# Key features of two batches in one block, joined GpSimd sums, and a factor moved to PSUM, in an attention and ELU kernel on one Trainium2 core

## The chip, the cores and the metric

The kernel runs on one core of a Trainium2 chip. The metric is the device time of one execution in microseconds. Before the change it is 264.04 us, the median of three runs (263.98 to 265.52).

## The reference

Two stages, all in float32 in effect (inputs that arrive in a wider type are rounded on the chip):

```python
def phi(x):                                    # r = 8
    a = einsum('rd,bhsd->bhsr', S1, x)
    b = einsum('rd,bhsd->bhsr', S2, x)
    return einsum('bhsi,bhsj->bhsij', a, b).reshape(..., 64)
q_p, k_p = phi(q), phi(k)                      # q, k, v: 4 batches, 4 heads, 1088 rows, 32 wide
kv = einsum('bhsf,bhsd->bhfd', k_p, v)
z  = sum(k_p, axis=2)
x  = einsum('bhsf,bhfd->bhsd', q_p, kv) / (einsum('bhsf,bhf->bhs', q_p, z) + 1e-6)
x  = x.transpose(0, 2, 1, 3).reshape(4352, 128)
h  = x @ w_in                                  # 128 -> 2048
g  = where(h > 0, h, exp(min(h, 0)) - 1)
out = g @ w_out                                # 2048 -> 128
```

## The kernel before, in words

The 4352 rows are cut into nine groups: groups 0 to 7 have 512 rows each (two to a batch), group 8 has the 256 left over. The 2048 hidden columns are cut into eight pairs `cp` of 128-column chunks. A step of the main loop (L1047) is one pair (group, cp), numbered n. Steps 2 to 15 take groups 0 and 1 alternately, steps 16 to 23 group 2, 24 to 31 group 3, 32 to 39 group 4, and so on to step 63; group 8 has a loop of its own at the end (L1090).

The schedule is written out by hand: each engine runs its instructions in the order in which the program issues them. A step n issues, in this order:

1. `mm1` (L787), TensorE: both halves c0 and c1 of h, 512 columns each, into two of the four banks of the PSUM tag `h`. So step n uses the banks of step n-2.
2. what was filed for the step with `at(n, ...)`.
3. `elu` of half 0: two ScalarE activations make e from h (L808, L810), one VectorE instruction makes gg from e and h (L816).
4. what was filed with `mid(n, ...)`.
5. `elu` of half 1.
6. what was filed with `late(n, ...)`.
7. the second matmul of step n-2, from its gg.

From step 14 on the second matmul is `mm2_seven` (L717), a scheme with seven products of half-size blocks in place of eight. Three of its operands are plain quarters of gg and the other four are sums of quarters, `tt` (t0 to t3), which GpSimd makes in `sums7` (L690): t0 after half 0, then t2, t1 (from t2) and t3 (from t1) after half 1. The products are issued as p1, p2, p3, p5 (t0), p7 (t2), p6 (t1), p4 (t3); in the first and last step of a group p6 and p3 come third and fourth.

The attention stage is spread over the same steps. For batches 1 to 3 the key side is: `transp` (L279) transposes the loaded keys on VectorE; `KF_late` (L353) computes the key features on TensorE, as eight matmuls on array tiles of 64 by 32, into two banks of the PSUM tag `aux` (two banks in all); `KF_late_out` (L365) empties them with two VectorE transposes into `abk`; `KO_a` and `KO_b` form the outer products (L378, L386); `KA` (L422) sums keys times values; `turn` and `turned` finish z. The loop at L993 files these under the steps in its table: `n_t` for the transpose, `n_f` for the key features.

The query side: `queries(g5, g1, n)` (L655) is a TensorE block in step n-1 that computes the numerators of group g5 (L642) and the query features of group g1 (L536), into the two h banks of step n and two `aux` banks (`qps`). In step 22 it does the numerators of group 3 and the features of groups 4 and 5. Before that, for group 3, `q2_den` (L555) makes the denominators on VectorE (pw, den, an), `q2_half` (L620) the outer product qp from an and abw (L625), and `q4` (L628) transposes qp. For groups 4 to 7 `q2_a` (L614) first copies an into an `aux` bank with ScalarE (tile `qa`), and `q2_half` reads it from there.

The buffers that matter: `kT` and `qT` have two buffers each, shared by batches 0 and 2 and by 1 and 3; `abk` has two; `gg` three; `tt` shares a tag of five.

Of the kernel before, what the change touches and what calls it, by code (L numbers as in the profile page):

```python
# [12 lines left out]
F32 = mybir.dt.float32  # L13
ALU = mybir.AluOpType
U32 = mybir.dt.uint32
MUL, ADD, SUB, MAX = ALU.mult, ALU.add, ALU.subtract, ALU.max
# [6 lines left out]
def _ap(ap: bass.AP, free):  # L23
    return dataclasses.replace(ap, ap=[list(ap.ap[0])] + [list(x) for x in free])
# [3 lines left out]
def kernel(  # L28
# [21 lines left out]
    nc = tc.nc  # L50
    B, H, S, D = q.shape
    R = S1.shape[0]
    P = 128
# [4 lines left out]
    NT = S // 64  # L58
# [7 lines left out]
    psum = ctx.enter_context(tc.tile_pool(name="psum", bufs=2, space=bass.MemoryType.PSUM))  # L66
# [5 lines left out]
    kT = [const.tile([FD, 2 * KT, 64], F32, name=f"kT{b}") for b in range(2)] * 2  # L72
    qT = [const.tile([FD, NT, 64], F32, name=f"qT{b}") for b in range(2)] * 2
# [276 lines left out]

    def KF_late(b):  # L353
        ps = [psum.tile([P, 512], F32, name="kfps", tag="aux") for _ in range(2)]
        for c in range(4):
            u, w = divmod(c, 2)
            for g2 in range(2):
                r = slice(64 * g2, 64 * g2 + 64)
                nc.tensor.matmul(ps[g2][32 * c:32 * c + 32, :32 * KT],  # L359
                                 Sxp[r].rearrange("p x c r -> p (x c r)"),  # L360
                                 kT[b][r, u * KT:u * KT + KT, 32 * w:32 * w + 32],
                                 skip_group_check=True, tile_position=(64 * g2, 32 * c))
        feats[b] = ps
# [303 lines left out]
    hs, es, gs, ops = {}, {}, {}, {}  # L667
# [19 lines left out]
    def quarter(g, cp, c, y):  # L687
        return gs[g, cp][:, c].rearrange("p (u x s) -> p u x s", u=2, x=2)[:, :, y, :]

    def sums7(g, cp, c):  # L690
        if c == 0:
            ts[g, cp] = work.tile([P, 4, 2, P], F32, name="tt", tag="raw", bufs=5)
        t = ts[g, cp]
        b11, b12 = (quarter(g, cp, 0, y) for y in range(2))
        if c == 0:
            nc.gpsimd.tensor_tensor(t[:, 0], b12, b11, op=SUB)  # L696
            return
        b21, b22 = (quarter(g, cp, 1, y) for y in range(2))
        nc.gpsimd.tensor_tensor(t[:, 2], b22, b12, op=SUB)  # L699
        nc.gpsimd.tensor_tensor(t[:, 1], t[:, 2], b11, op=ADD)  # L700
        nc.gpsimd.tensor_tensor(t[:, 3], b21, t[:, 1], op=SUB)  # L701

# [248 lines left out]
    steps = [(0, 0), (0, 1), (1, 0), (1, 1)] + [(g, cp) for cp in range(2, NP - 2) for g in range(2)]  # L951
# [6 lines left out]
    def at(n, f, *a):  # L958
        extra.setdefault(n, []).append((f, *a))

    def mid(n, f, *a):
        extra.setdefault((n, 0), []).append((f, *a))

    def late(n, f, *a):
        extra.setdefault((n, 1), []).append((f, *a))
# [25 lines left out]


    for b, (n_t, n_f, n_o, n_a, n_z) in enumerate(  # L993
            ((4, 6, (7, 9), 11, 12), (15, 16, (17, 18), 19, 20), (19, 21, (23, 24), 27, 28)), 1):
        at(n_t, transp, kT, "k", b, 0, NT)
        at(n_f, KF_late, b)
        late(n_f, KF_late_out, b)
        for half in range(2):
            if b == 1:
                at(n_o[half], KO, b, half, nc.gpsimd)  # L1000
            else:
                late(n_o[half] - 1, KO_a, b, half)
                at(n_o[half], KO_b, b, half)
        at(n_a, KA, b)
        late(n_a, sums_out, b)
        at(n_z, turn, b)
        at(n_z, turned, b)
    late(10, transp, qT, "q", 1, 0, NT)
    at(21, transp, qT, "q", 2, 0, NT)
    late(24, transp, qT, "q", 3, 0, NT)  # L1010

    for n, g, nx in ((13, None, 2), (15, 2, 3), (22, 3, 4), (30, 4, 6), (46, 6, 8), (62, 8, None)):
# [8 lines left out]
    late(13, q2_half, 2, 0)  # L1021
    mid(14, q4, 2)
    late(19, q2_den, 3)
    late(19, q2_half, 3, 0)
    late(20, q4, 3)
    late(22, q2_den, 4)
# [20 lines left out]
    for n in range(2, N):  # L1047
        g, cp = steps[n]
# [6 lines left out]
        if seven(g, cp):  # L1055
            sums7(g, cp, 0)
# [15 lines left out]
        if seven(g, cp):  # L1072
            sums7(g, cp, 1)
# [4 lines left out]
        g, cp = before  # L1078
# [10 lines left out]
    g = NQ - 2  # L1089
# [53 lines left out]
```

## Time and profile before

| | us |
|---|---|
| median of three runs | 264.04 |
| profiled execution, its own time | 264.85 |
| span of the profiled execution, first to last instruction | 262.9 |
| mean of one gg instruction (L816), 128 of them | 0.682 |
| mean of one GpSimd sum (L696, L699, L700, L701), 50 of each | 0.735, 0.737, 0.731, 0.760 |
| mean of one stored-key transpose of 1088 columns (L280) | 1.311 |

The profile is of one execution. Busy times of the engines overlap, and a share of the span is an average over stages. The engines are PE (TensorE; PEld is its weight loading, which overlaps), DVE (VectorE), ACT (ScalarE), POOL (GpSimd) and SP, which issues transfers. PE can count as busy while a matmul waits for its bank, so a wait of PE is looked for in the start times and in the weight loads, too. The granted TensorE clock has a mean of 0.998 of full speed.

### The profile page before, as it was taken

The numbers are of one execution on the slowest core, as the hardware profiler recorded it, in microseconds if no ns is written. First come the engines' busy times: TensorE is split into PE (matmuls) and PEld (weight loads), VectorE is DVE, ScalarE is ACT, GpSimd is POOL, SyncE is SP. The second block draws the span as 40 slices with busy tenths as digits, with TensorE's granted clock in tenths as the row PEclk, the third lists the DMA queues.
The fourth block names the chain that finished last, engine by engine and source line by source line (L and its number), as shares of the span: only waits on it lengthen the run. The fifth ranks groups of instructions, "written<-read, shape, count | busy, mean of one in ns | idle before, by whom it ended". The sixth has DMA issues, their size and how long they took to land.

```text
span 262.9 us, 9941 instructions
## 1 busy us (share of the span) xinstructions
PE 257.1 (98%) x4219; PEld 159.2 (61%) x4219; DVE 188.2 (72%) x355; ACT 182.9 (70%) x356; POOL 169.2 (64%) x253
## 2 busy tenths in 40 slices
PE   8899999999999999999999999999999999999994
PEld 6652333354346746667666666665666666667994
DVE  5899999997969997996477676644456445673651
ACT  2469878677567655784687777776777777777793
POOL 4420008205387996798868799898689888997300
PEclk9999999999999999999999999999999999999999
DMA  5998079012011210001100200011001100110021
GB/s 171 326 353 220 7 235 268 7 36 78 12 24 26 33 38 3 5 15 26 35 0 4 30 13 2 0 29 15 5 0 17 27 4 0 24 21 2 0 32 33
DMA packets 28507, 14.30 MB, mean 54 GB/s; under 512 B 21392, under 2 KB 26640, under 8 KB 28464
## 3 DMA queue, kind: packets, MB, share of 16 engines
q1 hardware_dynamic: 28032, 13.32, 20.6%
q8 instruction: 33, 0.54, 0.9%
q10 hardware_dynamic: 368, 0.30, 0.3%
q14 instruction: 10, 0.08, 0.1%
q0 software_dynamic: 64, 0.07, 0.1%
HBM read 11.31 MB, written 2.36 MB: 52 GB/s over the span
## 4 chain that ended last, share of the span: by engine, by line
PE 94%; DMA 2%; DVE 1%; ACT 0%; issue 0%; ACTq 0%; DVEq 0%
PE h L256 45%; PE pb L737 17%; PE pa L737 13%; PE o L256 5%; PE pb L713 4%; PE ol L256 3%; DMA hd_k<-in_k_dram 2%; PE h L642 1%; PE kv L427 1%; PE qps L642 1%; PE kfps L359 1%; PE h L536 1%; PE qtp L595 1%; DVE qp L583 0%; PE xps L602 0%; PE abp L340 0%
## 5 line engine op out<-in xcount | busy, mean ns | idle before, releaser
L256 PE MATMUL h<-xg,W 128*32 128x512 f32 (+3 forms) x904 | 130.9, 540 | 0.4 <-ACT xg L608 0.4
L816 DVE SCALAR_TENSOR_TENSOR gg<-e,h 128x512 f32<-128x512 f32 x128 | 85.5, 682 | 52.6 <-ACT e L810 51.3
L808 ACT ACTIVATE e<-h 128x512 f32<-128x512 f32 x128 | 75.5, 590 | 47.0 <-PE h L256 46.0
L810 ACT ACTIVATE e<-e 128x512 f32<-128x512 f32 x128 | 80.9, 632 | 3.8
L256 PEld LDWEIGHTS h<-xg,W 128*32 128x32 f32 (+1 forms) x904 | 43.1, 122 | 43.2 <-issue 34.0
L699 POOL TENSOR_TENSOR tt<-gg 128x256 f32<-128x256 f32 x50 | 36.8, 737 | 16.3 <-DVE gg L816 16.1
L696 POOL TENSOR_TENSOR tt<-gg 128x256 f32<-128x256 f32 x50 | 36.7, 735 | 6.5 <-DVE gg L816 6.2
L701 POOL TENSOR_TENSOR tt<-gg,tt 128x256 f32<-128x256 f32 x50 | 38.0, 760 | 3.9
L700 POOL TENSOR_TENSOR tt<-tt,gg 128x256 f32<-128x256 f32 x50 | 36.6, 731 | 3.9
L737 PEld LDWEIGHTS pa<-gg,W 128*64 128x64 f32 (+1 forms) x496 | 23.9, 126 | 23.7 <-issue 23.0
L737 PE MATMUL pa<-gg,W 128*64 128x128 f32 (+1 forms) x496 | 30.7, 274 | 0.0
L737 PE MATMUL pb<-tt,SS 128*64 128x128 f32 (+1 forms) x480 | 29.6, 273 | 0.0
L737 PEld LDWEIGHTS pb<-tt,SS 128*64 128x64 f32 (+1 forms) x480 | 22.8, 126 | 0.0
L737 PE MATMUL pa<-tt,SS 128*32 128x128 f32 (+1 forms) x288 | 21.2, 273 | 0.0
L737 PE MATMUL pb<-tt,W 128*64 128x128 f32 (+1 forms) x256 | 20.2, 273 | 0.2 <-issue 0.2
L737 PE MATMUL pb<-gg,SS 128*64 128x128 f32 (+1 forms) x256 | 19.9, 273 | 0.0
L134 POOL TENSOR_TENSOR raw<-raw,tiny 128x512 f32<-128x512 f32 x1 | 1.0, 1042 | 24.7 <-DVE raw L129 24.7
L256 PE MATMUL o<-gg,W 128*32 128x512 f32 x128 | 15.3, 595 | 0.0
L737 PEld LDWEIGHTS pa<-tt,SS 128*32 128x32 f32 (+1 forms) x288 | 13.7, 124 | 0.0
L737 PEld LDWEIGHTS pb<-tt,W 128*64 128x64 f32 (+1 forms) x256 | 12.8, 125 | 0.5 <-issue 0.5
L737 PEld LDWEIGHTS pb<-gg,SS 128*64 128x64 f32 (+1 forms) x256 | 12.8, 125 | 0.0
L713 PE MATMUL pb<-gg,W 128*32 128x256 f32 x192 | 11.6, 380 | 0.0
(154 smaller groups left out, 285.2 us busy)
## 6 DMA issues: line engine op xcount, KB each, us to landing
raw<-in_moe_w_in_dram SPq DMA_DIRECT2D x8, 256.0 KB, 6.3
raw<-in_moe_w_out_dram SPq DMA_DIRECT2D x8, 256.0 KB, 6.6
out_dram<-ob SPq DMA_DIRECT2D x112, 16.0 KB, 1.5
hd_k<-in_k_dram SPq DMA_DIRECT2D x3, 544.0 KB, 6.8
hd_q<-in_q_dram SPq DMA_DIRECT2D x3, 544.0 KB, 8.2
v<-in_v_dram SPq DMA_DIRECT2D x4, 288.0 KB, 7.0
v<-in_v_dram SPq DMA_DIRECT2D x4, 256.0 KB, 8.6
kvs<-kvd SPq DMA_DIRECT2D x13, 32.0 KB, 1.9
```

Source lines behind the costliest of these rows:

```text
L256: nc.tensor.matmul(dst[c:c + tile], lhs[:, c:c + tile], rhs, skip_group_check=True, tile_position=(0, c), **kw)
L359: nc.tensor.matmul(ps[g2][32 * c:32 * c + 32, :32 * KT], Sxp[r].rearrange("p x c r -> p (x c r)"), kT[b][r, u * KT:u * KT + KT, 32 * w:32 ...
L642: nc.tensor.matmul(ps[w][32 * r:32 * r + 32, :64 * n], kvs[b][rows, r, f, :], qpT[g, i][rows, o:o + 2 * n, f, :], start=(f == 0), stop=(f ...
L696: nc.gpsimd.tensor_tensor(t[:, 0], b12, b11, op=SUB)
L699: nc.gpsimd.tensor_tensor(t[:, 2], b22, b12, op=SUB)
L700: nc.gpsimd.tensor_tensor(t[:, 1], t[:, 2], b11, op=ADD)
L701: nc.gpsimd.tensor_tensor(t[:, 3], b21, t[:, 1], op=SUB)
L713: nc.tensor.matmul(acc[1][0][r:r + width[0], 256 * hi:256 * hi + 256], lhs[:, w:w + width[0]], gg[:, c, 256 * u:256 * u + 256], start=(cp ...
L737: nc.tensor.matmul(bank[r:r + width[0], P * col:P * col + P], lhs[:, w:w + width[0]], rhs[:, u], start=(first and i in ((0,) if g == 1 els ...
L808: nc.scalar.activation(e, hs[g, cp][c][:, :n], RELU, scale=-1.0)
L810: nc.scalar.activation(e, e, EXP, scale=-1.0)
L816: nc.vector.scalar_tensor_tensor(gs[g, cp][:, c, :n], es[g, cp][:, c, :n], -1.0, hs[g, cp][c][:, :n], op0=ADD, op1=MAX)
```

## The change

Four edits. The key features of batch 3 move from step 21 to step 16, right behind those of batch 2; they go into the two h banks of step 17 instead of `aux` banks, and are emptied between the two halves of step 16. The transposes of loads move with them: batch 2's keys from step 15 to the end of step 12, batch 3's keys from step 19 to step 15, batch 2's queries from step 21 to step 19. GpSimd's t0 and t2 become one instruction after half 1, so that each step has three GpSimd sums in place of four. And group 3's factor an is copied into an `aux` bank by ScalarE, as that of the later groups is.

```diff
-    def KF_late(b):
-        ps = [psum.tile([P, 512], F32, name="kfps", tag="aux") for _ in range(2)]
+    def KF_late(b, n=None):
+        if n is None:
+            ps = [psum.tile([P, 512], F32, name="kfps", tag="aux") for _ in range(2)]
+        else:
+            ps = hs[steps[n]] = [psum.tile([P, 512], F32, name="h", tag="h", bufs=4) for c in range(2)]
...
-        b11, b12 = (quarter(g, cp, 0, y) for y in range(2))
         if c == 0:
-            nc.gpsimd.tensor_tensor(t[:, 0], b12, b11, op=SUB)
             return
-        b21, b22 = (quarter(g, cp, 1, y) for y in range(2))
-        nc.gpsimd.tensor_tensor(t[:, 2], b22, b12, op=SUB)
+        b11, b21 = quarter(g, cp, 0, 0), quarter(g, cp, 1, 0)
+        us = [[2 * P, 2], [1, P]]
+        nc.gpsimd.tensor_tensor(_ap(t[:, 0], [[4 * P, 2], [P, 2], [1, P]]), _ap(gs[g, cp][:, 0, P:], [[4 * P, 2]] + us),
+                                _ap(gs[g, cp][:, 0], [[P, 2]] + us), op=SUB)
         nc.gpsimd.tensor_tensor(t[:, 1], t[:, 2], b11, op=ADD)
         nc.gpsimd.tensor_tensor(t[:, 3], b21, t[:, 1], op=SUB)
...
-            ((4, 6, (7, 9), 11, 12), (15, 16, (17, 18), 19, 20), (19, 21, (23, 24), 27, 28)), 1):
-        at(n_t, transp, kT, "k", b, 0, NT)
-        at(n_f, KF_late, b)
-        late(n_f, KF_late_out, b)
+            ((4, 6, (7, 9), 11, 12), (12, 16, (17, 18), 19, 20), (15, 16, (23, 24), 27, 28)), 1):
+        (late if b == 2 else at)(n_t, transp, kT, "k", b, 0, NT)
+        at(n_f, KF_late, b, n_f + 1 if b == 3 else None)
+        (mid if b == 3 else late)(n_f, KF_late_out, b)
...
-    at(21, transp, qT, "q", 2, 0, NT)
+    at(19, transp, qT, "q", 2, 0, NT)
...
     late(19, q2_den, 3)
+    late(19, q2_a, 3, 0)
     late(19, q2_half, 3, 0)
```

## Prediction

> **What bounds the kernel now.** I read the page's busy times first, then the chain of waits, then the four engines' timelines from 60 to 125 us, where everything that the change touches lies. "Step" is the index n of the step loop; c0 and c1 are the two halves of a step.
>
> ```profile
> span 262.9 us, 9941 instructions
> PE 257.1 (98%) x4219; PEld 159.2 (61%) x4219; DVE 188.2 (72%) x355; ACT 182.9 (70%) x356; POOL 169.2 (64%) x253
> ```
>
> PE is busy 98% of the span, and the chain of waits gives it 94%. A plain step is 1.72 us of `mm1` (L256) and 1.52 of seven products (L737): the starts 105.72, 108.97 and 112.21 are 3.24 apart. So only two kinds of edit can move the end: fewer PE instructions or changes of tile shape, and waits that hide inside "busy" PE. Timeline of PE, then its weight loads (start, duration, instruction; the bracket is a wait and what ended it):
>
> ```profile
> 92.45 1.94 PE L256 MATMUL h<-xg,W 128*32 128x512 f32 x16
> 94.32 0.71 PE L359 MATMUL kfps<-kT,Sxp 64*32 64x288 f32 x16
> 94.96 0.64 PE L737 MATMUL pa<-gg,W 128*32 128x128 f32 x16
> ...
> 98.35 0.65 PE L642 MATMUL h<-qpT,kvs 32*32 32x128 f32 x4
> 98.98 0.66 PE L642 MATMUL qps<-qpT,kvs 32*32 32x128 f32 x3
> ...
> 100.93 0.64 PE L737 MATMUL pa<-gg,W 128*32 128x128 f32 x16
> ```
>
> ```profile
> 98.98 0.13 PEld L642 LDWEIGHTS qps<-qpT,kvs 32*32 32x32 f32 x2 [0.26 <-DVE abk L369]
> 99.35 0.10 PEld L642 LDWEIGHTS qps<-qpT,kvs 32*32 32x32 f32 x1 [0.23 <-DVE abk L369]
> ```
>
> This is step 21 and the `queries` block of step 22. That block wants the two `aux` banks that `KF_late(3)` filled in step 21, and VectorE empties them (abk, L369) only at 98.47 to 99.29. It takes 100.93 - 98.35 = 2.58 us. The block of step 15 (three rounds of 128 columns, 71.06 to 72.47) takes 1.41, that of step 30 (three of 256, 128.81 to 130.87) 2.06; this one has two rounds of 128 and one of 256, so 1.41 + 0.65/3 = 1.63. The stall is 2.58 - 1.63 = 0.95 us. Why VectorE is late:
>
> ```profile
> 88.41 1.26 DVE L816 SCALAR_TENSOR_TENSOR gg<-e,h 128x512 f32<-128x512 f32 x2
> 89.58 0.24 DVE L436 STREAM_TRANSPOSE kvt<-kv 128x64 f32<-128x64 f32 x1
> 89.73 0.82 DVE L560 TENSOR_TENSOR pw<-abw 128x128 f32<-128x128 f32 x1
> 90.58 0.30 DVE L567 TENSOR_REDUCE den<-pw 128x16 f32<-128x144 f32 x1
> 90.92 0.25 DVE L568 RECIPROCAL den<-den 128x16 f32<-128x16 f32 x1
> 91.21 0.78 DVE L570 TENSOR_TENSOR an<-abw,den 128x128 f32<-128x128 f32 x1
> 92.02 1.71 DVE L625 TENSOR_TENSOR qp<-an,abw 128x1024 f32<-128x1024 f32 x1
> ...
> 94.94 1.23 DVE L632 STREAM_TRANSPOSE qpT<-qp 128x1024 f32<-128x1024 f32 x1
> 96.11 1.27 DVE L280 STREAM_TRANSPOSE qT<-hd_q 128x1088 f32<-128x1088 f32 x1
> 97.30 1.24 DVE L816 SCALAR_TENSOR_TENSOR gg<-e,h 128x512 f32<-128x512 f32 x2
> 98.47 0.82 DVE L369 STREAM_TRANSPOSE abk<-kfps 128x288 f32<-128x288 f32 x2
> ```
>
> Its timeline marks no idle time from 81.82 to 99.87. Three rows are long: the same pw and an took 0.28 and 0.29 in step 14 (66.17, 67.10), and qp took 1.23 there.
>
> **Part by part.** *Batch 3's key features in step 16.* Step 21 loses its block: `mm1` would end at 92.45 + 1.72 = 94.17, the products start at 94.96 (and run 0.03 longer), so 0.82 us. Of that, 288 columns at `mm1`'s rate (1.72 us for two rounds of 512) are 0.48; the rest is the change of tile shape. In step 16 the second block follows one of the same shape, so it adds 0.48, at most 0.64 (the block's own start to the next start). PE: -0.34. Its banks are step 17's h banks, read last by step 15's gg, which ends near 75.2, before PE gets there at 76.69. Their emptying (0.84) moves between step 16's two gg: PE is done near 77.17, gg c0 near 77.23, the transposes near 78.1; `mm1` of step 17 needs the banks at 78.24 + 0.48 = 78.72. Hidden by 0.6 us; beyond that PE waits one for one. Everything after is 0.48 later with PE.
>
> *The four transposes of loads.* Batch 2's keys (1.3 us) go into VectorE's idle 1.50 before gg at 64.16: free; without that gap gg of step 13 slips a few tenths, and PE wants its banks only at 69.2. Batch 3's keys take the old place of batch 2's, batch 2's queries that of batch 3's keys: equal lengths, nothing. What counts is that the 1.27 at 96.11 is gone. The loads were issued by SP at 33.57 to 36.09 and land a median 6.8 (keys) and 8.2 us (queries) later; no later load waits for the freed buffers, so SP's queue does not move.
>
> *The stall in step 22.* KF's two banks are out of the way, so the block waits only for gg of step 21 (its h banks). Now follow VectorE with the third edit, group 3's factor in PSUM. pw starts at 89.73 + 0.48 = 90.21; with the trace's own excess an ends at 90.21 + 2.26 = 92.47. A new wait follows: the ScalarE copy `qa` stands in ScalarE's queue ahead of step 20's two exponentials and waits for an. The same shape of handover (abk to ka to kp, 79.21 to 79.57) costs 0.36: qp starts at 92.83 and takes 1.18 (the rows that read qa: 1.18 at 115.07, 1.21 at 117.37), end 94.01, against 93.73 + 0.48 = 94.21 before. ScalarE is free at 92.78, so e of step 20 is there at 94.04 and 95.19 (1.26 and 2.41 after the start, as from 90.28); gg 20 ends 95.88 (`mm1` of step 22 needs it near 97.03); qpT to 97.0; e of step 21 at 97.5, gg 21 c1 ends near 98.2. PE reaches the block at 98.35 + 0.48 - 0.82 = 98.01: a stall of 0.2. Bounds: without any excess on pw and an, an ends at 91.43 and there is no stall; with a whole joined GpSimd sum (1.29, below) before each of the two, an ends at 90.21 + 1.22 + 2.58 = 94.0 and the stall is near 1.75. I take 0.2, the row's own excess.
>
> *GpSimd's sums joined.* GpSimd's rows grow evenly: 128x128 0.46, 128x192 0.60, 128x256 0.735, so 128x512 is 0.735 + 256 x 2.15 ns = 1.29; the one two-input 128x512 row (L135) is 1.31. Two sums of 0.735 become one of 1.29: 0.18 us less in each of 50 steps, 9 us off an engine that is not on the chain. But the sum on c0 no longer starts early, and the last result comes 1.29 - 0.735 = 0.55 later after gg c1. Cover, step by step: in a plain step t3 would be ready at 209.66 against a use at 211.99 or later; the tightest are step 23 (t1 ready 110.0, used 111.12) and the last step (t1 244.92, used 246.06), where 1.1 us shrinks to 0.6. Zero on the path; a further 0.6 of delay would make PE wait one for one. In step 19 the joined sum also meets VectorE:
>
> ```profile
> 89.67 0.73 POOL L701 TENSOR_TENSOR tt<-gg,tt 128x256 f32<-128x256 f32 x1
> 90.36 0.79 POOL L696 TENSOR_TENSOR tt<-gg 128x256 f32<-128x256 f32 x1
> 91.11 0.73 POOL L699 TENSOR_TENSOR tt<-gg 128x256 f32<-128x256 f32 x1
> 91.92 0.73 POOL L700 TENSOR_TENSOR tt<-tt,gg 128x256 f32<-128x256 f32 x1
> 92.73 1.60 POOL L701 TENSOR_TENSOR tt<-gg,tt 128x256 f32<-128x256 f32 x1
> ```
>
> pw, an and qp end 0.15, 0.15 and 1.08 us after a GpSimd sum has ended, and the sum at 92.73 lasts as long as qp. The Trainium skill, SBUF — State Buffer, "Who interferes with whom", says that a VectorE instruction with two SBUF inputs and a GpSimd instruction that reads SBUF exclude each other for a whole instruction, whoever starts first. That speaks against joining: by it the longest wait grows from 0.73 to 1.29, and with both waits at the longest the sum would be the upper bound above rather than the 0.2. It speaks for the factor in PSUM.
>
> Sum: -0.82 + 0.48 - 0.95 + 0.2 = -1.09 us. The profiled execution took 264.85 (span 262.9 and 1.95 around it), so it would take 263.76; it lies 0.81 above the median, and the median of 264.04 becomes 262.95, say 263.0.
>
> **Rivals.** *ScalarE's new wait (slower).* If an ends later than 92.47 + 1.09 = 93.56, the e of steps 20 and 21, held behind `qa`, make the block of step 22 wait over 1.3 us, and the kernel is slower than before. At the bound of 94.0: -0.34 - 0.95 + 1.75 = +0.46, 264.5. For it: both waits of VectorE are in the trace already and the sums get longer. Against: it needs two nearly full waits.
>
> *The wait stays in another form.* One full wait gives a stall near 0.95, and only PE's 0.34 is gained: 263.7. For it: gg of step 21 ends at 98.54 already in the trace.
>
> *GpSimd becomes the bound.* A step then costs the joined sum plus 1.62 (the starts 203.51, 204.32, 205.13 and 0.73). Above 1.62 us for the joined sum that exceeds 3.24; at 1.75 some 46 steps lose 0.13 each, 6 us, 270. Against: all widths of the trace lie on one line, and even two old sums end to end are 1.47.
>
> **How the numbers follow.** Forecast (262.7 to 263.4) 0.68, stall kept (263.4 to 263.9) 0.14, ScalarE's wait 0.12, GpSimd 0.04, and 0.02 for a larger gain than PE's idle time shows. Range: from the no-stall end, 264.04 - 1.29 = 262.75, less 0.25 for the scatter of the runs, to 264.2, inside the slower rival. One per cent, 2.6 us, is about what tells a difference from none; only GpSimd's rival reaches it: faster 0.02, same 0.94, slower 0.04.
>
> **What would show it.** Two kfps/h blocks of 0.64 + 0.48 back to back near 76; `mm1` of step 17 without a wait; no block in step 21; the queries block near 1.6 to 1.9 us, its wait now on gg; `qa` right behind an; qp near 1.2; the joined sum near 1.29 and the seven products every 3.24 us. Wrong if the products wait for tt, or if PE waits over 1.3 us in step 22.

## The result and the profile after

| | before | after |
|---|---|---|
| median of eleven runs each, us | 264.07 | 263.41 |
| lowest and highest | 263.75, 265.76 | 263.0, 263.75 |
| profiled execution, its own time | 264.85 | 263.75 |
| its span | 262.9 | 261.9 |

The ratio is 0.9964, with a 95% interval of 0.9947 to 0.9981: between 0.5 and 1.4 us less. The forecast was 263.0, inside a range of 262.5 to 264.2, and "no change beyond 1%" had 0.94. The part of the range that had 0.68 ends at 263.4, so 263.41 lies just above it, in the part of the rival "stall kept"; the timelines below show that the stall was not kept. The two profiled executions differ by 1.10 us against a working of 1.09. That fit is closer than the working deserves, as the ledger below shows.

The head of the page after the change:

```profile
span 261.9 us, 9901 instructions
PE 256.3 (98%) x4219; PEld 160.3 (61%) x4219; DVE 188.5 (72%) x355; ACT 183.1 (70%) x357; POOL 161.3 (62%) x203
...
L701 POOL TENSOR_TENSOR tt<-gg 128x512 f32<-128x512 f32 x50 | 64.3, 1285 | 29.8 <-DVE gg L819 23.5
```

GpSimd is busy 161.3 us instead of 169.2, with 50 instructions fewer; the joined sum takes 1.285 us. PE makes the same 4219 matmuls. The timeline of PE in steps 16, 21 and 22 (start, duration, instruction):

```profile
76.08 0.71 PE L362 MATMUL kfps<-kT,Sxp 64*32 64x288 f32 x16
76.59 0.69 PE L362 MATMUL h<-kT,Sxp 64*32 64x288 f32 x16
77.21 0.42 PE L740 MATMUL pa<-gg,W 128*32 128x128 f32 x8
...
78.77 1.90 PE L256 MATMUL h<-xg,W 128*32 128x512 f32 x16
...
93.28 1.89 PE L256 MATMUL h<-xg,W 128*32 128x512 f32 x14
94.79 0.70 PE L740 MATMUL pa<-gg,W 128*32 128x128 f32 x14
...
96.52 1.89 PE L256 MATMUL h<-xg,W 128*32 128x512 f32 x14
98.34 0.40 PE L645 MATMUL h<-qpT,kvs 32*32 32x128 f32 x2
...
100.05 0.65 PE L740 MATMUL pa<-gg,W 128*32 128x128 f32 x16
```

In step 16 the two blocks of key features follow each other, in step 21 there is none between `mm1` and the products, and the queries block of step 22 takes 100.05 - 98.34 = 1.71 us instead of 2.58. No wait for `abk` is left in it. The timeline of VectorE from step 19's gg to step 21's:

```profile
88.93 1.26 DVE L819 SCALAR_TENSOR_TENSOR gg<-e,h 128x512 f32<-128x512 f32 x2
90.10 0.23 DVE L439 STREAM_TRANSPOSE kvt<-kv 128x64 f32<-128x64 f32 x1
90.25 0.41 DVE L563 TENSOR_TENSOR pw<-abw 128x128 f32<-128x128 f32 x1
...
91.31 1.39 DVE L573 TENSOR_TENSOR an<-abw,den 128x128 f32<-128x128 f32 x1
93.04 1.23 DVE L628 TENSOR_TENSOR qp<-qa,abw 128x1024 f32<-128x1024 f32 x1 [0.34 <-ACT qa L621]
...
95.38 0.69 DVE L819 SCALAR_TENSOR_TENSOR gg<-e,h 128x512 f32<-128x512 f32 x1 [0.39 <-ACT e L813]
95.98 1.24 DVE L635 STREAM_TRANSPOSE qpT<-qp 128x1024 f32<-128x1024 f32 x1
97.14 1.25 DVE L819 SCALAR_TENSOR_TENSOR gg<-e,h 128x512 f32<-128x512 f32 x2
```

And GpSimd's, beside an:

```profile
91.28 1.28 POOL L701 TENSOR_TENSOR tt<-gg 128x512 f32<-128x512 f32 x1
92.63 0.73 POOL L703 TENSOR_TENSOR tt<-tt,gg 128x256 f32<-128x256 f32 x1
```

Where before pw took 0.82, an 0.78 and qp 1.71, now pw takes 0.41, an 1.39 and qp 1.23. an stands next to a whole joined sum: it begins 0.03 us after it and ends 0.14 after its end, as pw and an did with the short sums. That is what the Trainium skill, SBUF — State Buffer, "Who interferes with whom", says of such a pair (one excludes the other for a whole instruction), and here it costs 1.39 - 0.29 = 1.10 us of VectorE's time. qp, which now reads its factor from PSUM, does not stretch, although a sum runs beside it from 92.63.

**A ledger by steps.** For all kernels, the start of each step's `mm1` minus the start of step 16's was compared with the profile of before; the differences are the change in length of each stretch, in us. Steps not named agree within 0.07 for all kernels but one (`e9_pool256`). "End" is the start of the last step of the main loop. "Median" is the median's distance from the kernel before on the same chip (of one run each for the last two).

| kernel | step 16 | steps 19 to 22 | step 27 | step 30 | end | median |
|---|---|---|---|---|---|---|
| changed kernel | +0.50 | -1.41 | -0.11 | -0.06 | -1.06 | -0.66 |
| e1_features | +0.49 | -1.73 | +0.10 | -0.05 | -1.18 | -0.89 |
| e2_sums | 0 | +0.21 | -0.37 | 0 | -0.15 | +0.15 |
| e3_psum | 0 | +0.30 | -0.29 | 0 | +0.02 | +0.32 |
| e4_no_psum | +0.49 | -1.70 | -0.45 | -0.07 | -1.73 | -1.24 |
| e5_no_sums | +0.49 | -1.56 | +0.30 | -0.06 | -0.80 | -0.93 |
| e6_queries21 | +0.49 | -1.52 | -0.45 | -0.07 | -1.51 | -1.16 |
| e7_empty_late | +1.40 | -1.40 | -0.46 | -0.08 | -0.51 | -0.04 |
| e8_pool64 | +0.50 | -1.73 | -0.24 | -0.06 | -1.52 | -1.51 |
| e10_den18 | +0.49 | -0.58 | -0.23 | -0.06 | -0.37 | -0.09 |
| e11_again | +0.49 | -1.59 | -0.11 | -0.06 | -1.24 | -1.20 |
| e12_no_out2 | +0.49 | -1.61 | -0.12 | -0.06 | -1.28 | -1.23 |

With step 21's -0.82 and the whole stall, steps 19 to 22 could give at most -1.77. Step 27 is no part of the change: there PE waits 0.43 us in the profile before, and between nothing and 0.73 in the others. The experiments show below that it differs between two executions of one kernel. Without it the ledger reads +0.50 - 1.41 - 0.06 = -0.97 for the changed kernel; the medians' interval holds that and the forecast.

### The profile page after: what moved, and what is told of

The parts are those of the page before. It is cut to its first block, busy times and chain, and to the rows that moved or that the text cites. A ratio compares the mean times of both kernels' runs of the same rounds, so it can differ in the third digit from the quotient of the medians.

```text
span 261.9 us, 9901 instructions
## 1 busy us (share of the span) xinstructions
PE 256.3 (98%) x4219; PEld 160.3 (61%) x4219; DVE 188.5 (72%) x355; ACT 183.1 (70%) x357; POOL 161.3 (62%) x203
## 4 chain that ended last, share of the span: by engine, by line
PE 97%; DVE 1%; ACT 0%; issue 0%; DVEq 0%
PE h L256 45%; PE pb L740 17%; PE pa L740 13%; PE o L256 5%; PE pb L716 4%; PE ol L256 3%; PE idle L264 1%; PE kv L430 1%; PE h L645 1%; PE abp L340 1%; PE h L539 1%; PE qps L645 1%; PE qtp L598 1%; DVE qp L586 0%; PE xps L605 0%; PE kfps L362 0%
## 5 line engine op out<-in xcount | busy, mean ns | idle before, releaser
L701 POOL TENSOR_TENSOR tt<-gg 128x512 f32<-128x512 f32 x50 | 64.3, 1285 | 29.8 <-DVE gg L819 23.5
L704 POOL TENSOR_TENSOR tt<-gg,tt 128x256 f32<-128x256 f32 x50 | 36.9, 738 | 3.9
L871 DVE SCALAR_TENSOR_TENSOR gg<-e,h 128x256 f32<-128x256 f32 x16 | 6.6, 418 | 6.4 <-PE h L256 3.2
```

Of the source, the lines that this page charges most:

```text
L701: nc.gpsimd.tensor_tensor(_ap(t[:, 0], [[4 * P, 2], [P, 2], [1, P]]), _ap(gs[g, cp][:, 0, P:], [[4 * P, 2]] + us), _ap(gs[g, cp][:, 0], [[ ...
L871: nc.vector.scalar_tensor_tensor(gs["last", k // 2][:, k % 2, :2 * P], es["last", k // 2][:, k % 2, :2 * P], -1.0, hs["last", k][:, :2 * P ...
```

## The experiments

Theory at the start: the gain is the move of batch 3's key features (PE's time and the stall), while the joined sums and the factor in PSUM bring nothing. Rivals: the factor in PSUM is needed to get rid of the stall, or a lighter GpSimd is.

**The parts alone.** `e1_features` is the moves alone: the changed kernel with the old four sums and without the line for `q2_a`. `e5_no_sums` is the changed kernel with the old four sums. `e2_sums` and `e3_psum` are the kernel before with one part each:

```diff
# e2_sums
...
-            nc.gpsimd.tensor_tensor(t[:, 0], b12, b11, op=SUB)
...
-        nc.gpsimd.tensor_tensor(t[:, 2], b22, b12, op=SUB)
...
+        nc.gpsimd.tensor_tensor(_ap(t[:, 0], [[4 * P, 2], [P, 2], [1, P]]), _ap(gs[g, cp][:, 0, P:], [[4 * P, 2]] + us),
+                                _ap(gs[g, cp][:, 0], [[P, 2]] + us), op=SUB)
# e3_psum
     late(19, q2_den, 3)
+    late(19, q2_a, 3, 0)
```

> Batch 3's key features in step 16 and the three moved transposes alone; four GpSimd sums, group 3's factor in SBUF. Theory (the gain is PE's 0.33 us and the freed wait of step 22): without the copy ahead of step 20's exponentials gg of step 21 ends near 97.9 us, before PE reaches the queries block near 98.04, so that nothing is left of the wait: span 262.9 - 0.33 - 0.95, near 261.6, and 1.1 to 1.3 us below the kernel before. Rival (GpSimd's relief or the factor in PSUM made part of the gain): at most 0.5 below the kernel before.

> The kernel before with t0 and t2 in one GpSimd instruction, nothing else. Theory: GpSimd is off the path, and the longer sum can only make VectorE's an of step 19 later: 0 to +0.5 us against the kernel before, GpSimd 8 us less busy. Rival (GpSimd's relief is part of the gain): 0.3 us or more below the kernel before.

> The kernel before with group 3's factor copied to PSUM, nothing else. Theory: qp is 0.5 us shorter, but begins 0.36 us later, and the copy holds the exponentials of step 20, so that step 20's second gg ends some 0.4 us later than before and all behind it on VectorE with it: 0 to +0.4 us against the kernel before. Rival (the factor in PSUM freed step 22): 0.3 us or more below it.

> The changed kernel with the four GpSimd sums of before. Theory: an of step 19 (1.39 us in the changed kernel, behind a whole joined sum) waits at most 0.5 us, gg of step 21 ends 0.2 to 0.7 us earlier, and the 0.28 us left of step 22's wait goes in part: 0 to 0.3 us below the changed kernel. Rival (GpSimd's relief counts): 0.2 us or more above it.

Measured, against a median of 264.32 before: `e1_features` 263.43, ratio 0.9962 (0.9949 to 0.9975); `e2_sums` 264.47, 1.0004 (0.9996 to 1.0013); `e3_psum` 264.64, 1.0009 (1.0001 to 1.0018); `e5_no_sums` 263.39, 0.9963 (0.9951 to 0.9975). The moves alone give the ratio of the whole change. `e1_features` on VectorE, then on PE:

```profile
92.31 1.71 DVE L628 TENSOR_TENSOR qp<-an,abw 128x1024 f32<-128x1024 f32 x1
...
96.41 1.24 DVE L819 SCALAR_TENSOR_TENSOR gg<-e,h 128x512 f32<-128x512 f32 x2
```

```profile
97.86 0.30 PE L645 MATMUL h<-qpT,kvs 32*32 32x128 f32 x2
...
99.49 0.64 PE L740 MATMUL pa<-gg,W 128*32 128x128 f32 x16
```

Here pw, an and qp take 0.82, 0.77 and 1.71, as long as before the change. Still gg of step 21 is done at 97.65, before PE gets to the block at 97.86, and the block takes 99.49 - 97.86 = 1.63 us: there is no stall. The factor in PSUM was not needed, and neither were the joined sums.

The two other parts each make step 22 longer, by 0.21 and 0.30. In `e2_sums` an meets a whole joined sum (1.39, as in the changed kernel) and everything behind it is late. In `e3_psum` the hand-over costs, on ScalarE and then on VectorE:

```profile
91.69 0.27 ACT L618 COPY qa<-an 128x128 f32<-128x128 f32 x1 [3.67 <-DVE an L570]
```

```profile
91.99 1.23 DVE L625 TENSOR_TENSOR qp<-qa,abw 128x1024 f32<-128x1024 f32 x1 [0.34 <-ACT qa L618]
...
94.32 0.69 DVE L816 SCALAR_TENSOR_TENSOR gg<-e,h 128x512 f32<-128x512 f32 x1 [0.39 <-ACT e L810]
```

qp is 0.48 shorter, but VectorE waits 0.34 for the copy and 0.39 for the exponential that stood behind the copy in ScalarE's queue: together more than it saves. In the medians these losses are at the edge of what can be told (the interval of `e3_psum` begins at 1.0001).

**The change without one part.** `e4_no_psum` leaves out the factor's move; `e10_den18` brings the denominators one step forward, away from the tight stretch:

```diff
# e4_no_psum
-    late(19, q2_a, 3, 0)
# e10_den18
-    late(19, q2_den, 3)
+    late(18, q2_den, 3)
```

> The changed kernel with group 3's factor left in SBUF (features moved and sums joined). Theory: an still ends near 92.7 us behind the joined sum, qp takes 1.7 in place of 0.34 + 1.2, but no exponential is held, so that gg of step 21 ends at about 98.0 to 98.4 and the queries block of step 22 waits 0 to 0.3 us: within 0.3 us of the changed kernel. Rival (the factor in PSUM is what frees step 22): 0.5 us or more above the changed kernel.

> The changed kernel with group 3's denominators one step earlier (end of step 18 in place of 19), so that an is there before the copy's turn. Theory (what is left of step 22's wait, 0.28 us, comes from the copy that waits for an and holds step 20's exponentials): VectorE loses its idle 0.34 and 0.39 us around qp and the first gg of step 20, gg of step 21 ends before PE arrives, and the kernel is 0 to 0.3 us below the changed one. Rival (VectorE's plain amount of work sets it): no change.

`e4_no_psum`: 262.95 against 264.19, ratio 0.9953 (0.9936 to 0.997). an takes 1.40 and qp 1.70, yet gg of step 21 ends at 97.77, just as PE reaches the block of step 22, and the block takes 1.66 us. The rival (0.5 us or more above) is out. It has the lowest time of all parts and combinations of the change, but its interval overlaps that of the changed kernel, so it is not shown to be faster.

`e10_den18`: 264.10 against 264.19, ratio 0.9998 (0.9987 to 1.0009). Step 22 loses its whole stall (-0.95), and a new one of 1.20 us stands in step 20. The timeline of VectorE, then of the weight loads:

```profile
88.44 1.32 DVE L573 TENSOR_TENSOR an<-abw,den 128x128 f32<-128x128 f32 x1
89.67 1.30 DVE L280 STREAM_TRANSPOSE qT<-hd_q 128x1088 f32<-128x1088 f32 x1
90.90 1.24 DVE L819 SCALAR_TENSOR_TENSOR gg<-e,h 128x512 f32<-128x512 f32 x2
92.07 0.22 DVE L439 STREAM_TRANSPOSE kvt<-kv 128x64 f32<-128x64 f32 x1
```

```profile
92.35 0.16 PEld L256 LDWEIGHTS kv<-zl,SXh 128*32 128x32 f32 x8 [1.86 <-DVE kvt L439]
```

The denominators and the queries' transpose now both stand ahead of gg of step 19 and of `kvt`, and PE waits for `kvt`, since its next product overwrites the bank that `kvt` reads. VectorE has as much to do as before, only with another deadline first. Both the theory (0 to 0.3 us below the changed kernel) and its rival (no change) missed this: the run has no gain over the kernel before, and its interval lies apart from that of the changed kernel.

**Was it the queries' transpose?** The prediction said of the four transposes that "what counts is that the 1.27 at 96.11 is gone". `e6_queries21` puts just that one back:

```diff
-    at(19, transp, qT, "q", 2, 0, NT)
+    at(21, transp, qT, "q", 2, 0, NT)
```

> The changed kernel with the transpose of batch 2's queries back in step 21. Theory: gg of step 21 ends 1.2 us later (97.14 to 98.39 becomes about 99.6), the queries block waits for it, and 1.0 to 1.2 us are lost against the changed kernel, so about as slow as the kernel before. Rival (only the aux banks of the key features held the block): no change against the changed kernel.

Measured: 263.03 against 264.19, ratio 0.9956 (0.994 to 0.9971). The expected loss of over 1 us did not come. VectorE in `e6_queries21`:

```profile
89.08 0.27 DVE L563 TENSOR_TENSOR pw<-abw 128x128 f32<-128x128 f32 x1
...
90.01 0.29 DVE L573 TENSOR_TENSOR an<-abw,den 128x128 f32<-128x128 f32 x1
...
94.75 1.30 DVE L280 STREAM_TRANSPOSE qT<-hd_q 128x1088 f32<-128x1088 f32 x1
95.94 1.28 DVE L819 SCALAR_TENSOR_TENSOR gg<-e,h 128x512 f32<-128x512 f32 x2
```

The transpose is back in front of gg, and gg of step 21 still ends early. The two profiles are shifted against each other by 0.49 us at step 16, ahead of everything compared here, so times are compared by their distance from the start of step 16's `mm1`, in the changed kernel and in `e6_queries21`:

```profile
74.25 1.90 PE L256 MATMUL h<-xg,W 128*32 128x512 f32 x16
```

```profile
73.76 1.90 PE L256 MATMUL h<-xg,W 128*32 128x512 f32 x16
```

gg of step 21 ends 23.46 us behind it, against 24.14 in the changed kernel, and PE reaches the block only at 24.08. Without the transpose in step 19, pw begins 0.68 us earlier (15.32 against 16.00). That is less than a whole transpose, since gg of step 19 then waits 0.40 for its exponential. And at that moment no sum of GpSimd is in the way of pw and an: 0.27 and 0.29 in place of 0.41 and 1.39, 1.24 us less. Together this is more than the 1.19 that the transpose costs ahead of gg of step 21. So its place bought nothing here, and that is in part the phase of GpSimd's sums. With batch 3's keys moved to step 15, steps 19 to 21 hold one transpose of loads instead of two, wherever it stands; that and the emptying of batch 3's banks are what the change took out of the stretch. The expectation had overlooked that step 19 is then without one.

The outcome, no change, is the one that the rival named. That the `aux` banks alone held the block is not shown by it: no run frees the banks with both transposes still in steps 19 to 21, so what each of the two gave stays open.

**The emptying.** `e7_empty_late` empties batch 3's features at the end of step 16 instead of between its halves:

```diff
-        (mid if b == 3 else late)(n_f, KF_late_out, b)
+        late(n_f, KF_late_out, b)
```

> The changed kernel with batch 3's key features emptied at the end of step 16 and no longer between its halves. Theory: their two transposes come after gg c1 and after batch 2's two, to about 80.0 us, while mm1 of step 17 wants the first bank at 78.77: PE waits 0.8 us there, of which up to 0.28 comes back in step 22: 0.5 to 0.9 us above the changed kernel. Rival (PE has slack there): no change.

Measured: 264.15 against 264.19, ratio 0.9997 (0.9986 to 1.0008). The weight loads of `e7_empty_late`:

```profile
79.13 0.16 PEld L256 LDWEIGHTS h<-xg,W 128*32 128x32 f32 x8 [0.98 <-DVE abk L372]
```

Step 16 grows by 1.40 in place of 0.49: `mm1` of step 17 waits for the second pair of transposes. In the changed kernel that pair runs first, from 77.44 to 78.29, and `mm1` of step 17 begins at 78.77, so 0.48 us of cover were there. Without the filing between the halves, one word of the edit, the medians show no gain at all.

**GpSimd's margin.** Two kernels give GpSimd more to do in every step, with a sum whose result nothing reads, of width 64 in `e8_pool64` and of 256 in `e9_pool256`:

```diff
+    spare = const.tile([P, 64], F32, name="spare")
...
+        nc.gpsimd.tensor_tensor(spare[:], t[:, 0].rearrange("p u s -> p (u s)")[:, :64], t[:, 2].rearrange("p u s -> p (u s)")[:, :64], op=ADD)
         nc.gpsimd.tensor_tensor(t[:, 1], t[:, 2], b11, op=ADD)
```

> The changed kernel with one more GpSimd sum of 128x64 in each step, between the joined sum and t1, whose result nobody reads. It takes some 0.3 us, so that a step of GpSimd grows from 2.9 to 3.2 us and t1 and t3 come 0.3 us later, with 0.6 us of slack at the tightest place. Theory: 0 to 0.2 us above the changed kernel. Rival (GpSimd's results are already what PE waits for): 2 us or more above it.

> The same with a spare sum of 128x256, 0.81 us from start to start: GpSimd's step is 3.7 us, above PE's 3.24. Theory: GpSimd becomes the bound, PE waits for tt in the second half of the kernel, and the time grows by 10 to 20 us. Rival (GpSimd is never on the path): under 1 us.

Measured against 264.41: `e8_pool64` 262.90, ratio 0.994 (0.9925 to 0.9956); `e9_pool256` 272.65, ratio 1.0306 (1.0285 to 1.0328). GpSimd in a plain step of `e9_pool256`, and one weight load:

```profile
201.10 1.28 POOL L702 TENSOR_TENSOR tt<-gg 128x512 f32<-128x512 f32 x1
202.46 0.73 POOL L704 TENSOR_TENSOR spare<-tt 128x256 f32<-128x256 f32 x1
203.15 0.73 POOL L705 TENSOR_TENSOR tt<-tt,gg 128x256 f32<-128x256 f32 x1
203.95 0.73 POOL L706 TENSOR_TENSOR tt<-gg,tt 128x256 f32<-128x256 f32 x1
204.64 1.28 POOL L702 TENSOR_TENSOR tt<-gg 128x512 f32<-128x512 f32 x1
```

```profile
110.97 0.16 PEld L742 LDWEIGHTS pa<-tt,SS 128*32 128x32 f32 x8 [0.81 <-POOL tt L705]
```

That is 8.2 us above the kernel before on the same chip and some 9 above the changed kernel on another, a little under what was expected: the spare sum and t1 don't depend on each other and start 0.69 apart. A round of GpSimd takes 204.64 - 201.10 = 3.54 us, 0.30 over PE's step of 3.24, and PE waits for tt: against the kernel before, nearly all of its steps 36 to 45 and 52 to 61 are 0.2 to 0.35 longer. This fits the threshold where the prediction put it, at a round of 3.24. A round of the changed kernel in which GpSimd has no gap, 112.97 - 110.09 = 2.88 (the starts of two joined sums in its timeline; the shortest are 2.85), lies 0.36 below. `e8_pool64`, with shortest rounds of 3.13, is not slower. Its steps 19 to 22 give -1.73: pw and an take 0.28 and 0.29 there, because they come first and GpSimd's sums beside them stretch instead (0.77 and 0.89 for 0.73). Its median is the lowest of all, with an interval that overlaps that of the changed kernel; it is a matter of phase, and nothing in it promises to survive the next edit.

**Step 27.** `e5_no_sums` lost 0.73 us in step 27, where the profile before shows 0.43. `e11_again` is the same kernel once more; `e12_no_out2` is that kernel without the sixteen transfers that write group 2's output, which are under way then:

```diff
-                    for w in range(2):
+                    for w in range(2 if g != 2 else 0):
```

> The same kernel as e5_no_sums once more, for the wait of PE in step 27 that no record releases (0.43 us in the profile of before, 0.32 after, 0.73 in e5_no_sums, about 0 in e4 to e7). If the wait belongs to the program, it is again 0.6 us or more; if it belongs to the single execution, it is another value between 0 and 0.7.

> e5_no_sums without the 16 output transfers of group 2 (those rows of the output are left unwritten), which SP issues while PE is in step 27. If the wait of step 27 comes from PE's instructions being fetched beside these transfers, it falls from 0.73 us to under 0.2; if it comes from the instruction sequence itself, it stays at 0.6 or more.

Measured once each, beside 264.28 before: 263.08 and 263.05, with a wait in step 27 of 0.32 and 0.31 us. The same kernel shows 0.73 in one execution and 0.32 in another, so the length of the wait does not belong to the program; the two ran on different chips, so it may be the chip's or the execution's. Without the transfers the wait is still there, as long as with them on that chip, so they are not needed for it. What causes it stays open.

## Why the prediction was right, and where its steps were not

- **The features' move on PE** (-0.82 + 0.48): the ledger gives -0.82 in step 21 and +0.49 to +0.50 in step 16. The low end for the second block was the right one: here the block behind another of its shape costs its columns (0.48 by the working) and no change of shape.
- **The stall** (-0.95, of which 0.2 stays): right in mechanism and near in size. The block takes 1.71 instead of 2.58 and waits for gg of step 21, not for `abk`; 1.71 - 1.63 leaves 0.08 of stall. PE came to it at 98.34, 0.33 later than the 98.01 of the working. Some 0.2 of that is a delay which PE took along from step 19 (last section), and it hid part of the wait: gg of step 21 ends at 98.39 against 98.2 in the working. By the ledger steps 19 to 22 give -1.41, where the working had -0.82 - 0.95 + 0.2 = -1.57.
- **The path through VectorE**: the sum was near, its terms were not. an was to end at 92.47 "with the trace's own excess" and ended at 92.70; but pw lost only 0.13 and an a whole joined sum, 1.10, where the working had 0.54 and 0.49. qp started at 93.04 (92.83 in the working) and took 1.23 (1.18). The excess is no property of the instruction. It depends on where GpSimd's round stands at that moment, and the bounds (0 to 1.75 us of stall) said so better than the value taken.
- **"What counts is that the 1.27 at 96.11 is gone"**: right as a sum, wrong as a place. `e6_queries21` put that transpose back at 94.75, right ahead of gg of step 21, at no loss. What counts, by the timelines, is VectorE's whole work from step 19 on: the change leaves one transpose of loads there instead of two (1.3 us less), and takes the two of the emptying (0.82) out from behind gg of step 21.
- **The factor in PSUM** was given a part in the sum (qp ends 94.01 in place of 94.21). Its own effect is a loss of 0.30 in step 22 (`e3_psum`), and without it the change has its whole gain (`e4_no_psum`). The working counted the hand-over of 0.36, which came out at 0.34, and the held exponential (e at 95.19, so gg of step 20 ends 95.88; measured 96.06). But it compared only the end of qp with the trace before. Without the copy gg of step 20 would have ended at 95.02 + 0.48 = 95.50, so its own numbers made the move a loss of 0.38 at that gg.
- **The joined sum** (1.29 us, zero on the path): measured 1.285, and the plain steps are as long as before, without a wait for tt, so the halved cover held. In step 22 it is not zero: +0.21 in `e2_sums`, through an.
- **The emptying hidden by 0.6**: 0.48 of cover in the profile after, and `e7_empty_late` shows the price without it.
- **The rivals**: ScalarE's wait needed an after 93.56, and it came at 92.70; the wait in another form needed some 0.95, and 0.08 was left; GpSimd's round stayed at 2.88 against 3.24.
- **The total**: the profiled executions' -1.10 holds 0.11 of step 27's chance, and without it the ledger's -0.97 is 0.12 short of the working. The medians' -0.66 is less than the 1.09 of the working, but their interval (0.5 to 1.4) holds it.

## What to carry to other kernels

When a bank or an operand waits for an engine that runs one queue in order, count all the work of that queue ahead of the deadline, not the instruction that stands last; moving one within the stretch bought nothing here, and moving another stretch's work away from it can break an earlier deadline. An instruction's excess over its undisturbed time through contention is a matter of phase: bound it by a whole instruction of the other engine from one side and by nothing from the other, and don't carry the measured excess over to a schedule that is shifted. Compare two profiles by distances from an event that both have, not by the times as they stand. Here a lighter engine that is not on the chain gave nothing, and its longer instructions made others wait longer.

## What the runs showed of the hardware

PE sometimes stops for a few tenths of a us in the products behind a burst of many small matmuls (`KA`), and nothing in the trace accounts for it (0 to 0.73 us in step 27 of the kernels here). The weight loads of step 27 in `e5_no_sums`:

```profile
117.94 0.28 PEld L740 LDWEIGHTS pa<-tt,SS 128*32 128x32 f32 x8
119.00 0.22 PEld L740 LDWEIGHTS pb<-tt,W 128*32 128x32 f32 x8 [0.78 <-POOL tt L704]
```

The same in `e6_queries21`, which does not stop, and GpSimd's t3 there:

```profile
117.86 0.28 PEld L740 LDWEIGHTS pa<-tt,SS 128*32 128x32 f32 x8
118.08 0.28 PEld L740 LDWEIGHTS pb<-tt,W 128*32 128x32 f32 x8
```

```profile
118.17 0.74 POOL L704 TENSOR_TENSOR tt<-gg,tt 128x256 f32<-128x256 f32 x1
```

The profile of `e5_no_sums` names a sum of GpSimd as the releaser. But in `e6_queries21` the same products load their weights at 118.08, before the round's t3 has even begun, so that sum is not one they need (they use the gg of two steps earlier); and in `e11_again` the wait at the same place is put down to "issue". Step 19, which also follows such a burst, has a smaller one in the changed kernel, on PE:

```profile
89.44 0.59 PE L740 MATMUL pb<-tt,W 128*32 128x128 f32 x6
89.74 0.62 PE L256 MATMUL h<-xg,W 128*32 128x512 f32 x2
89.86 0.28 PE L740 MATMUL pb<-tt,W 128*32 128x128 f32 x2
89.97 1.89 PE L256 MATMUL h<-xg,W 128*32 128x512 f32 x14
```

Two matmuls of the next step run ahead of the last two products, and the last fourteen begin 0.23 behind them. The same stagger goes on in the rows up to step 22 (the `mm1` rows of 14 above). `e5_no_sums` and `e6_queries21` show it too; `e1_features`, `e4_no_psum`, `e8_pool64` and `e11_again` do not. The `mm1` of step 20 in `e11_again`, the same kernel as `e5_no_sums`, is whole:

```profile
89.12 1.94 PE L256 MATMUL h<-xg,W 128*32 128x512 f32 x16
```

So the stagger, like the wait of step 27, is not fixed by the program. It also enters the ledger. Counted from the start of step 16's `mm1`, PE reaches the block of step 22 at 23.83 or 23.84 in the four named without the stagger, at 24.01 to 24.09 in the three with it. The products behind the block start at 25.46 in `e1_features`, where gg of step 21 ends at 23.62; at 25.61 in `e11_again`, where it ends at 23.94 and the block waits for it; at 25.71 in `e6_queries21`, with the stagger and gg at 23.46; and at 25.80 in the changed kernel, with the stagger and gg at 24.14. So differences of 0.1 to 0.2 us between these kernels in steps 19 to 22 are not all effects of their edits.
